# An S4 and spatial-shift mixer kernel: third-order norm roots, the last group's second stage per token row, transfers in two pieces of 64 partitions with all stores on SyncE, fewer idle products

## The chip, the cores and the metric

One core of a Trainium2 chip runs the kernel. The metric is the device time of one execution in microseconds; where several runs are given it is their median. TensorE (PE) multiplies matrices, VectorE (DVE) and ScalarE (ACT) work on tiles, and SyncE (SP) issues transfers, which 16 DMA engines carry out. ACT can issue transfers too.

## The reference

The input is A_u, 2048 tokens of D = 512 numbers. It is normalised per token, goes through a state-space convolution (N = 128 states per channel) and, beside it, through a mixer, and the two are multiplied and added to the input:

```python
def _A_ref(u, ...):                       # 2048-tap convolution by channel
    dt = jnp.exp(log_dt)[:, None]
    P = jnp.exp((dt * A)[:, :, None] * l[None, None, :])       # D x N x L
    K = jnp.einsum("dn,dnl,dn->dl", Cc, P, dt * Bc).real
    y = irfft(rfft(u padded) * rfft(K padded))[:L]
    return y + u * Dskip

def _B_ref(x, w1, w2, w3, w4):
    h = _gelu(_layernorm(x) @ w1)
    # quarters of the channels shifted by +1, -1, +2, -2 tokens
    x1 = x + shifted(h) @ w2
    return x1 + _gelu(_layernorm(x1) @ w3) @ w4                # F = 1376

xn = _layernorm(A_u)
s, g = _A_ref(xn, ...), _silu(_B_ref(xn, w1, w2, w3, w4))
return A_u + s * g
```

## The kernel before

The tile X holds all tokens: partition 64a + 32b + t, and on the free side s = 0 to 15 and the 512 channels. A token's row number in DRAM is made of (t, r, s) with r = 2b + a, so a block of 32 partitions belongs to one r; `ORDER = 0, 2, 1, 3` gives the r of each block.

The work has these stages. `loads` brings in X, the weights and the parameters. X is normalised row by row (s by s): sums of each row (`BN_STATS` to `stats`, `BN_AGGR` to `mv`), a reciprocal root (`rstd`, which takes Newton steps from a first guess), and an affine step. The normalised rows are transposed (xT) and go through w1 and w2 (the products `pb<-xT,w`, `pd<-w,hT`). Beside this the convolution's kernel is made from complex exponentials (`pt`, `mag`, `par`), and both are transformed in stages with scratch in DRAM (`scr_Ud`, `scr_Kda`, `scr_Zda` and others, reloaded as `uin`, `kin`, `zin`). Then the second mixing, `mlp(g)`, runs over groups of two rows s; its products are `pb<-x1T,w3h` and, summed over eleven blocks of F into two accumulators, `pa<-w4h,ghl`, one accumulator for each of the group's two rows. x1T is its transposed input. `inverse` makes the convolution's result from `zin` (products `pd<-zin,is` and `pc<-zin,is`). In `gate`, `inverse` and `finish` the group's X becomes silu(X), is multiplied by the convolution's result, gets the input added (loaded a second time as `xr`, four rows s at a time), and is stored. For the last group `pieces` splits these steps by row, for the others both rows go together.

Every operation is first recorded in a plan. `DUE`, one number for each operation, is the order of priority, and `PIN` says for the operations that ACT or DVE may do which of the two does them; a planner puts the operations of each engine in order by these. Each engine then works through its own list strictly in that order. `E.store` is such a choice too, between SP's queue and ACT's. Where the planner expects PE to wait over 0.8 us, it puts idle products (`pa<-ident`, `pd<-ident`, result not used) ahead of the next operation:

```python
pick.fill = max(0, int((t - start - LEFT) / SPAN))
```

All engines' operations are issued from one helper line, L499 in the kernel before; idle products come from L498. The DMAs on SP share eight semaphores, so a new transfer can be issued when the one eight places earlier has landed.

Of the kernel before, what the change touches and what calls it, by code (L numbers as in the profile page):

```python
# [14 lines left out]
ALU = mybir.AluOpType  # L15
# [9 lines left out]
S = 16  # L25
# [6 lines left out]
INV_2PI = float(np.float32(1.0 / (2.0 * np.pi)))  # L32
QUARTER_PI = float(np.float32(np.pi / 4.0))
# [63 lines left out]
class Op:  # L97
# [20 lines left out]
SPAN, LEFT, LEAST = 0.224, 0.3, 0.8  # L118
# [517 lines left out]
def kernel(  # L636
# [163 lines left out]
    def rstd(dst, var, x, t, by=1.0):  # L800
        V.tensor_scalar(x, var, EPS, None, op0=ALU.add)
        guess(dst, x)
        for f in (1.0, 1.0, by):
            V.scalar_tensor_tensor(t, dst, -0.5 * f, dst, op0=ALU.mult, op1=ALU.mult)
            V.tensor_mul(t, t, x)
            V.scalar_tensor_tensor(dst, t, 1.5 * f, dst, op0=ALU.add, op1=ALU.mult)
# [773 lines left out]
```

## Time and profile before

| what | value |
|---|---|
| time, median of 3 runs | 535.5 us (535.47 to 535.63) |
| the profiled execution's own time | 537.38 us |
| its span | 535.6 us |
| PE busy | 511.1 us, 95% |
| DVE busy | 450.9 us, 84% |
| ACT busy | 400.8 us, 75% |
| DMA on SP's queue | 106.95 MB |
| DMA on ACT's queue | 1.57 MB |
| chain that ended last | PE 68%, DVE 10%, ACT 10%, DMA 7% |

The profile is of one execution; its times are microseconds from the start of its span. The execution's own time is 1.8 us longer than the span, as it includes what lies around it. In a group row, "x16" is the number of instructions, and the name "out<-in" has the program's tiles. "DMA share" is the mean busy share of the 16 DMA engines, PEclk the granted clock of PE.

### The profile page before, as it was taken

How to read it: one execution, taken by the hardware profiler on the slowest of the kernel's cores; microseconds unless marked ns; L12 is line 12 of the kernel's file. 1: busy time of each engine (PE TensorE's matmuls, PEld its weight loads, DVE VectorE, ACT ScalarE, POOL GpSimd, SP SyncE). 2: the span in 40 equal slices, each digit the busy share in tenths (PEclk: the TensorE clock that was granted, in tenths of full speed). 3: DMA queues.
4: the chain of work that ended last, by engine and by line, in shares of the span. 5: the costliest groups of instructions: out<-in, count | busy, mean ns of one | idle time of the engine just before them, and what ended most of it. 6: DMA issues, size and time to landing. Idle time of an engine off the chain costs nothing.

```text
span 535.6 us, 14336 instructions
## 1 busy us (share of the span) xinstructions
PE 511.1 (95%) x6055; PEld 333.1 (62%) x6055; DVE 450.9 (84%) x783; ACT 400.8 (75%) x597; POOL 0.7 (0%) x6
## 2 busy tenths in 40 slices
PE   8789999999999999999999999999999999999992
PEld 8776666774343666565676676666655666566650
DVE  6899999999999999999999999999553267754593
ACT  4999999999998999998989999885336315322420
POOL 0000000000000000000000000000000000000000
PEclk9899999999999999999999999999999999999997
DMA  7994689983886506456333643547989859979986
GB/s 192 258 222 160 227 249 254 281 233 121 296 269 221 101 7 163 140 194 178 112 129 70 180 158 107 118 164 207 251 332 320 282 175 286 258 234 275 310 252 186
DMA packets 95329, 109.44 MB, mean 204 GB/s; under 512 B 40289, under 2 KB 74337, under 8 KB 94369
## 3 DMA queue, kind: packets, MB, share of 16 engines
q1 hardware_dynamic: 94592, 106.95, 69.4%
q10 hardware_dynamic: 672, 1.57, 1.0%
q8 instruction: 47, 0.77, 0.6%
q14 instruction: 18, 0.14, 0.1%
HBM read 64.46 MB, written 37.75 MB: 191 GB/s over the span
## 4 chain that ended last, share of the span: by engine, by line
PE 68%; DVE 10%; ACT 10%; DMA 7%; issue 2%; SPq 2%; ACTq 0%; DVEq 0%
PE pb L499 22%; PE pa L499 22%; PE pd L499 13%; PE pc L499 11%; DVE pt L499 7%; DMA X<-in_A_u_dram 4%; ACT pt L499 3%; SPq L499 2%; ACT ue L499 2%; DVE X L499 1%; ACT L496 1%; DMA scr_Ud<-ue 1%; ACT wst L499 1%; DMA cst<-c_gp 1%; DMA rawC<-in_A_B_re_dram 1%
## 5 line engine op out<-in xcount | busy, mean ns | idle before, releaser
L499 PE MATMUL pb<-x1T,w3h 128*128 128x256 f16 (+1 forms) x1056 | 124.9, 273 | 0.0
L499 PE MATMUL pa<-w4h,ghl 128*128 128x512 f16 (+1 forms) x528 | 123.4, 380 | 0.0
L499 PEld LDWEIGHTS <-w3h 128*128 128x128 f16 (+1 forms) x1056 | 102.6, 100 | 28.8 <-issue 11.6
L499 PEld LDWEIGHTS <-ghl 128*128 128x128 f16 (+1 forms) x528 | 49.4, 98 | 60.6 <-issue 9.2
L499 ACT ACTIVATE g<-pb,wsc 128x512 f32<-128x512 f32 (+1 forms) x48 | 30.7, 650 | 47.6 <-PE pb L499 43.6
L499 ACT ACTIVATE pt<-pt 128x2048 f32<-128x2048 int32 x32 | 61.0, 1908 | 2.4 <-DVE pt L499 2.3
L496 ACT ACT_TABLE_LOAD x48 | 61.6, 1283 | 1.6 <-PEq L1568 0.7
L499 DVE TENSOR_TENSOR pt<-mag,pt 128x1024 f32<-128x1024 f32 x48 | 58.1, 1215 | 0.1
L499 PE MATMUL pd<-w,hT 128*128 128x512 f32 x116 | 53.3, 600 | 2.4 <-DVE X L499 1.9
L499 DVE SCALAR_TENSOR_TENSOR ghl<-g,wsc,ghl 128x512 f16<-128x512 f32 (+1 forms) x48 | 33.5, 700 | 11.6 <-ACT ghl L499 11.3
L499 ACT ACTIVATE mag<-par 128x128 f32<-128x128 f32 x160 | 41.1, 463 | 0.1
L499 ACT ACTIVATE ghl<-g,wsc 128x512 f16<-128x512 f32 (+1 forms) x35 | 24.0, 688 | 20.5 <-PE pa L499 19.0
L499 PEld LDWEIGHTS pd<-w,hT 128*128 128x128 f32 x116 | 21.1, 190 | 27.7 <-issue 23.3
L499 DVE TENSOR_TENSOR pt<-pt 128x2048 f32<-128x2048 f32 x16 | 36.4, 2281 | 0.9 <-ACT pt L499 0.9
L499 PEld LDWEIGHTS pc<-pt 128*32 128x32 f32 x2048 | 29.5, 110 | 8.4 <-issue 5.8
L499 PE MATMUL pc<-pt 128*32 128x64 f32 x2048 | 32.4, 220 | 1.9 <-DVE pt L499 1.0
L499 ACT ACTIVATE pt<-pt,halfpi 128x2048 f32<-128x2048 f32 x16 | 32.0, 1999 | 0.1
L499 PE MATMUL pb<-xT,w 128*128 128x256 f32 x128 | 29.6, 383 | 1.4 <-ACT xT L499 1.4
L499 DVE TENSOR_TENSOR pr<-pd,uin 128x1024 f32<-128x1024 f32 x16 | 19.3, 1219 | 11.5 <-PE pd L499 11.5
L499 PEld LDWEIGHTS pb<-xT,w 128*128 128x128 f32 x128 | 23.6, 190 | 7.8 <-ACT xT L499 3.3
L499 DVE TENSOR_TENSOR pr<-pd,kh 128x1024 f32<-128x1024 f32 x16 | 19.3, 1218 | 6.7 <-PE pd L499 6.0
L499 PE MATMUL pb<-xT,w1h 128*128 128x256 f16 x192 | 22.5, 273 | 0.0
(160 smaller groups left out, 787.8 us busy)
## 6 DMA issues: line engine op xcount, KB each, us to landing
wst<-in_B_w_dram SPq DMA_DIRECT2D x20, 512.0 KB, 5.1
scr_Ud<-ue SPq DMA_DIRECT2D x16, 512.0 KB, 3.9
uin<-scr_Ud SPq DMA_DIRECT2D x32, 256.0 KB, 4.3
cst<-c_gp SPq DMA_DIRECT2D x16, 384.0 KB, 4.0
scr_Uh<-uh SPq DMA_DIRECT2D x8, 512.0 KB, 3.2
scr_Kfa<-k1e SPq DMA_DIRECT2D x8, 512.0 KB, 3.7
kin<-scr_Kfa SPq DMA_DIRECT2D x16, 256.0 KB, 4.1
scr_Zda<-z1e SPq DMA_DIRECT2D x8, 512.0 KB, 5.0
```

The costliest lines, as they stand in the source:

```text
L496: self.engines["ACT"].preload_act_table_set(SETS[table])
L499: ins = [getattr(self.engines[op.eng], name)(*args, **kw).ins for name, args, kw in op.calls]
```

## The change

1. `rstd` takes one third-order step and one Newton step instead of three Newton steps: 7 operations on DVE after the guess instead of 9, in each of eleven calls.
2. The row number is now split as (t, b, a, s), and X, xr and the stores move in two pieces of 64 partitions (one for each a) instead of four of 32. The side in DRAM is then 2 blocks (b) of 32 rows (t). X takes 10 transfers instead of 20, xr 8 instead of 16, the stores 18 instead of 36.
3. All stores are issued by SP; `E.store` is no longer used.
4. In the last group's second stage, the products into the accumulator of the first row are recorded ahead of those of the second row for each block, not alternating, and may be ordered apart.
5. The idle products are counted with a factor of 0.87: 50 instead of 57.
6. `DUE` and `PIN` have other numbers. They set the new order, and some operations go from ACT to DVE.

```diff
+CUBIC = 0.375 ** 0.5, -1.25 / 0.375 ** 0.5, 1.875
...
-SPAN, LEFT, LEAST = 0.224, 0.3, 0.8
+SPAN, LEFT, LEAST, FILLED = 0.224, 0.3, 0.8, 0.87
...
-                    pick.fill = max(0, int((t - start - LEFT) / SPAN))
+                    pick.fill = max(0, int((t - start - LEFT) * FILLED / SPAN))
...
-    xv = u[0].rearrange("(t r s) d -> r t s d", r=4, s=S)
-    ov = out[0].rearrange("(t r s) d -> r t s d", r=4, s=S)
+    xv = u[0].rearrange("(t b a s) d -> a b t s d", a=2, b=2, s=S)
+    ov = out[0].rearrange("(t b a s) d -> a b t s d", a=2, b=2, s=S)
...
-        for f in (1.0, 1.0, by):
-            V.scalar_tensor_tensor(t, dst, -0.5 * f, dst, op0=ALU.mult, op1=ALU.mult)
-            V.tensor_mul(t, t, x)
-            V.scalar_tensor_tensor(dst, t, 1.5 * f, dst, op0=ALU.add, op1=ALU.mult)
+        V.scalar_tensor_tensor(t, dst, CUBIC[0], dst, op0=ALU.mult, op1=ALU.mult)
+        V.tensor_mul(t, t, x)
+        V.scalar_tensor_tensor(t, t, CUBIC[1], t, op0=ALU.add, op1=ALU.mult)
+        V.scalar_tensor_tensor(dst, t, CUBIC[2], dst, op0=ALU.add, op1=ALU.mult)
+        V.scalar_tensor_tensor(t, dst, -0.5 * by, dst, op0=ALU.mult, op1=ALU.mult)
+        V.tensor_mul(t, t, x)
+        V.scalar_tensor_tensor(dst, t, 1.5 * by, dst, op0=ALU.add, op1=ALU.mult)
...
     def by_r(sb, dr, to_dram=False):
-        for r in range(4):
-            a, d = sb[32 * r : 32 * r + 32], dr[ORDER[r]]
-            Q.dma_start(d, a) if to_dram else Q.dma_start(a, d)
+        for a in range(2):
+            part = sb[64 * a : 64 * a + 64]
+            Q.dma_start(dr[a], part) if to_dram else Q.dma_start(part, dr[a])
...
-        for x, k in pieces(g):
-            V.tensor_add(X[:, x], X[:, x], xr[q][:, 2 * (g % 2) : 2 * (g % 2) + 2][:, k])
-            for r in range(4):
-                E.store(ov[ORDER[r]][:, x], X[32 * r : 32 * r + 32, x])
+        for x, k, c in pieces(g):
+            V.tensor_add(X[:, x, c], X[:, x, c], xr[q][:, 2 * (g % 2) : 2 * (g % 2) + 2][:, k, c])
+            by_r(X[:, x, c], ov[:, :, :, x][..., c], True)
...
-                with plan.together(cost=DOWN):
-                    for i in range(2):
-                        for lg, lw in ((0, 0), (0, 1), (1, 0)):
-                            T.matmul(accs[i], ...)
+                for some in ((0,), (1,)) if g == GROUPS[-1] else ((0, 1),):
+                    with plan.together(cost=DOWN * len(some) / 2):
+                        for i in some:
+                            for lg, lw in ((0, 0), (0, 1), (1, 0)):
+                                T.matmul(accs[i], ...)
```

In the lists below a row is an instruction with its output and input, the shape of the output, and the number in a row; numbers in names tell buffers apart (w_106 to w_109 are halves of w1 and w2). First, SP in the head, where X, the weights (wst, w) and the parameter Dt are loaded. Before:

```order
L499 DMA X<-in_A_u_dram 32x2048 x5
L499 DMA w_106<-in_B_w_dram 128x2x512
L499 DMA w_107<-in_B_w_dram 128x2x512
L499 DMA X<-in_A_u_dram 32x2048 x2
L499 DMA Dt<-in_A_Dskip_dram 1x2x64
L499 DMA wst<-in_B_w_dram 128x4x256
L499 DMA X<-in_A_u_dram 32x2048
L499 DMA Dt<-in_A_Dskip_dram 1x2x64
L499 DMA X<-in_A_u_dram 32x2048
L499 DMA is_82<-c_is 128x32
L499 DMA X<-in_A_u_dram 32x2048
```

After:

```order
L497 DMA w_107<-in_B_w_dram 128x2x512
L497 DMA X<-in_A_u_dram 64x1x2048 x2
L497 DMA w_106<-in_B_w_dram 128x2x512
L497 DMA X<-in_A_u_dram 64x1x2048
L497 DMA is_82<-c_is 128x32
L497 DMA X<-in_A_u_dram 64x1x2048
L497 DMA Dt<-in_A_Dskip_dram 1x2x64
L497 DMA w_109<-in_B_w_dram 128x2x512
L497 DMA Dt<-in_A_Dskip_dram 1x2x64
L497 DMA X<-in_A_u_dram 64x1x2048
```

Each X transfer now fills 64 partitions instead of 32, there are half as many, and their place among the weights is much the same.

Second, SP at the end, from the loads of xr to the last store. Before:

```order
L499 DMA xr<-in_A_u_dram 32x2048 x5
L499 DMA scr_Zdb<-z1e 128x1024
L499 DMA zin<-scr_Zda 128x4x256
L499 DMA xr<-in_A_u_dram 32x2048
L499 DMA zin<-scr_Zdb 128x4x256 x2
L499 DMA zin<-scr_Zda 128x4x256
L499 DMA zin<-scr_Zdb 128x4x256 x3
L499 DMA xr<-in_A_u_dram 32x2048
L499 DMA zin<-scr_Zdb 128x4x256
L499 DMA xr<-in_A_u_dram 32x2048
L499 DMA zin<-scr_Zdb 128x4x256 x2
L499 DMA zin<-scr_Zda 128x4x256
```

After:

```order
L497 DMA scr_Zdb<-z1e 128x1024
L497 DMA xr<-in_A_u_dram 64x1x2048 x3
L497 DMA zin<-scr_Zda 128x4x256
L497 DMA xr<-in_A_u_dram 64x1x2048
L497 DMA scr_Zdb<-z1e 128x1024
L497 DMA xr<-in_A_u_dram 64x1x2048
L497 DMA zin<-scr_Zda 128x4x256
L497 DMA zin<-scr_Zdb 128x4x256 x8
L497 DMA zin<-scr_Zda 128x4x256
L497 DMA out_dram<-X 2x32x1024 x14
L497 DMA out_dram<-X 2x32x512 x4
```

All loads of xr now stand ahead of ten of the eleven zin loads; before, three were among them. SP's list before ends with 22 stores of 32x1024 and 32x512; now it ends with 18 whose shape in DRAM is 2x32x1024 or 2x32x512.

Third, ACT at the end. Before:

```order
L499 DMA out_dram<-X 32x1024
L499 ACTIVATE ghl<-g_485,wsc 128x512
L499 ACTIVATE ghl<-g_487,wsc 96x256
L496 ACT_TABLE_LOAD
L499 ACTIVATE warm<-g_487 96x1
L499 DMA out_dram<-X 32x1024 x5
L499 ACTIVATE X<-X 128x512 x2
L499 DMA out_dram<-X 32x1024
L499 DMA out_dram<-X 32x512
L499 DMA out_dram<-X 32x1024
L499 DMA out_dram<-X 32x512 x3
```

After:

```order
L497 ACTIVATE ghl<-g_485,wsc 128x512
L497 ACTIVATE g_487<-pb_100,wsc 96x256
L494 ACT_TABLE_LOAD
L497 ACTIVATE warm<-g_487 96x1
L497 ACTIVATE ghl<-g_487,wsc 96x256
L497 ACTIVATE X<-X 128x512 x2
```

The stores are gone from ACT's list, which now ends with the last group's two functions.

More of the change, by code (lines that the diff above doesn't have):

```diff
@@ L226 @@
 PIN = (
-    "10111111111111111111111111111111111111111111111110101101101111111100111110010011101111111111101110100000111111"
-    "11111001111100100111011111111111110111111111111111111111111111101011011010101111111111111111111111111111111111"
-    "01110110110101011111111111111111111111101111111011011010111111101101101010111111111111111111111111111101111111"
-    "11111111111111111011010111111111110110101111111111111111111111111111110011111110110101010110111101101010111111"
-    "11111111010101010101010101010101111111111111111111111101101111111111111111111111111111111111111111111111111101"
@@ L232 @@
-    "11111111111111111111111111101101111111111111111111111111111111111111111011011111111111111111111101101111101111"
-    "10111110111110111110111110111110111110111110100110011010000000001111110001111111101111111000111111111111111100"
-    "01111111101111111000111111110101000000000111111000111111110111111100011111111011111110001111111101111111000111"
-    "11111011101111110111111001110111001111001111100111101111110011111001111100111001100111100111110011110111111111"
-    "01111001111100111001111111101111110111111101111110111111101111110111111101111110111111101111110111111101111110"
@@ L237 @@
-    "11111110111111011111110111111010100000000011111100011111111011111110001111111101111111000111111110111111100011"
-    "11111111010000000001111110001111111111111111000111111110111111100011111111011111110001111111101110011111001111"
-    "10111110111111110111111001111001111100111110011111001110011001111001111100111100111110011111001111101111011101"
-    "11110111111001111001111100111110111111011110111101111011111100111101111110011111001111100111111100111100111110"
-    "01111001111100111110011111011111100111110011110011011111111011110011100111011111111111110111111111110111111111"
@@ L242 @@
-    "11111111111111011111111111011111111111011111111111111111111111010000000001111111111111111111111111111111111111"
-    "111111111111111100111111011111111110110111111101101011111111001100111100"
+    "10111111111111111111111111111111111111101101011011111111001111100100111011111111111011101110001111111111100111"
+    "11001001110111111111011111010111111111111111111011111011011010101111111111111111111111111111111111110110110101"
+    "01111111111111111111111111111010110110101111111011011010101111111111111111111111111110011111111111111111111110"
@@ new lines @@
+    "11010111111111110110101111111111111111111111111110001111111011010101011011110110101011111111111111010101010101"
+    "01010101010111111111111111111111110110111111111111111111111111111111111111111111111101111111111111111111111111"
+    "10110111111111111111111111111111111111111011011111111111111111110110110110111110111110111110111110111110111110"
+    "11111011111010011001101000000000111111000111111110111111100011111111111111110001111111101111111000111111110101"
+    "00000000011111100011111111011111110001111111101111111000111111110111111100011111111011101111110111111001110011"
@@ new lines @@
+    "00111101111110111110011111011111101111110011100110011110111111001111001111111110111001111100111001111111101111"
+    "11011111110111111011111110111111011111110111111011111110111111011111110111111011111110111111011111111111111010"
+    "10000000001111110001111111101111111000111111110111111100011111111011111110001111111101010000000001111110001111"
+    "11110111111100011111111011111110001111111101111111000111111110111001111101111110111111110111110111111001111001"
+    "11110011111001111101111101100111100111110111110011111001111100111110111110110011110011111001111011111101111110"
@@ L244 @@
+    "11111101111011111111101111110111110111111011111100111110011111110111110111111001111001111101111111101111111101"
+    "11111110111111110011111100111011111111011110111101111001111111111110111111111110111111111111111111111110111111"
+    "11111111111111111011111111111111111111111110000000001111111111111111111111111111111111111111111111111111111111"
+    "1111111111111111111111111"
 )
@@ L832, in loads @@
     def loads():
-        by_r(X[:, 0:2], xv[:, :, 0:2])
+        by_r(X[:, 0:2], xv[:, :, :, 0:2])
         load_w(w1, w1s, stile)
@@ L842, in loads @@
         for k, (s0, s1) in enumerate(((2, 4), (4, 8), (8, 12), (12, 16))):
-            by_r(X[:, s0:s1], xv[:, :, s0:s1])
+            by_r(X[:, s0:s1], xv[:, :, :, s0:s1])
         load_w(w2, w2s, w2place)
@@ L1192, in gate @@
     def gate(g):
-        for x, _ in pieces(g):
-            A.activation(X[:, x], X[:, x], AF.Silu)
+        for x, _, c in pieces(g):
+            A.activation(X[:, x, c], X[:, x, c], AF.Silu)
     def inverse(hf, g):
@@ L1209, in inverse @@
                 return
-            for x, k in pieces(g):
-                V.tensor_mul(X[:, x], X[:, x], pair[:, k])
+            for x, k, c in pieces(g):
+                V.tensor_mul(X[:, x, c], X[:, x, c], pair[:, k, c])
             return
@@ L1221, in finish @@
             xr[q] = at(xrs.pop(), [P, 4, D], F32, "xr")
-            by_r(xr[q], xv[:, :, 4 * q : 4 * q + 4])
-        for x, k in pieces(g):
-            V.tensor_add(X[:, x], X[:, x], xr[q][:, 2 * (g % 2) : 2 * (g % 2) + 2][:, k])
-            for r in range(4):
-                E.store(ov[ORDER[r]][:, x], X[32 * r : 32 * r + 32, x])
+            by_r(xr[q], xv[:, :, :, 4 * q : 4 * q + 4])
+        for x, k, c in pieces(g):
+            V.tensor_add(X[:, x, c], X[:, x, c], xr[q][:, 2 * (g % 2) : 2 * (g % 2) + 2][:, k, c])
+            by_r(X[:, x, c], ov[:, :, :, x][..., c], True)
     def pow2_scale(cols, dst_s, dst_inv, target):
@@ L1443, in pieces @@
         if g != GROUPS[-1]:
-            return [(slice(2 * g, 2 * g + 2), slice(0, 2))]
-        return [(2 * g + k, k) for k in range(2)]
+            return [(slice(2 * g, 2 * g + 2), slice(0, 2), slice(0, D))]
+        return [(2 * g + k, k, slice(0, D)) for k in range(2)]
     def mlp(g):
@@ L1476, in mlp @@
                 fn = FT[j][1]
-                with plan.together(cost=DOWN):
-                    for i in range(2):
-                        for lg, lw in ((0, 0), (0, 1), (1, 0)):
-                            T.matmul(
-                                accs[i], ghl[:fn, lg, a, i * P : (i + 1) * P], w4t[jp][:fn, a, lw],
-                                start=j == 0 and lg == 0 and lw == 0,
-                                stop=j == len(FT) - 1 and lg == 1,
-                            )
+                for some in ((0,), (1,)) if g == GROUPS[-1] else ((0, 1),):
+                    with plan.together(cost=DOWN * len(some) / 2):
+                        for i in some:
+                            for lg, lw in ((0, 0), (0, 1), (1, 0)):
+                                T.matmul(
+                                    accs[i], ghl[:fn, lg, a, i * P : (i + 1) * P], w4t[jp][:fn, a, lw],
+                                    start=j == 0 and lg == 0 and lw == 0,
+                                    stop=j == len(FT) - 1 and lg == 1,
+                                )
         if g == GROUPS[-1]:
             A.activation(warm[:fr], g32[:fr, 0, 0:1], AF.Silu)
-        for x, k in pieces(g):
-            V.scalar_tensor_tensor(X[:, x], duo[0][:, k], a4, X[:, x], op0=ALU.mult, op1=ALU.add)
+        for x, k, c in pieces(g):
+            V.scalar_tensor_tensor(X[:, x, c], duo[0][:, k, c], a4, X[:, x, c], op0=ALU.mult, op1=ALU.add)
     def token_mixing():
```

179 rows, old and new, of the table DUE are left out of this document.

## The prediction

> **What bounds the kernel now.** I read the page first, then the busy times by stretch, then the tensors whose transfers change, then the chain at the end.
>
> ```profile
> span 535.6 us, 14336 instructions
> PE 511.1 (95%) x6055; PEld 333.1 (62%) x6055; DVE 450.9 (84%) x783; ACT 400.8 (75%) x597; POOL 0.7 (0%) x6
> core 0: us, PE busy (x) PEld busy (x) DVE busy (x) ACT busy (x) POOL busy (x), PEclk, DMA share, GB/s
> 0.00:40.00 40.00, 33.36 (x224) 30.71 (x224) 33.83 (x123) 32.77 (x87) 0.70 (x6) 0.96 0.96 224
> 40.00:180.00 140.00, 133.64 (x1535) 83.00 (x1536) 137.89 (x266) 136.18 (x188) 0.00 (x0) 1.00 0.78 226
> 180.00:370.00 190.00, 189.76 (x2644) 124.61 (x2643) 186.25 (x264) 175.60 (x255) 0.00 (x0) 1.00 0.47 134
> 370.00:525.00 155.00, 154.15 (x1656) 94.82 (x1653) 89.73 (x129) 55.05 (x69) 0.00 (x0) 1.00 0.89 269
> 390.00:400.00 10.00, 10.00 (x80) 5.52 (x68) 5.62 (x9) 3.23 (x4) 0.00 (x0) 1.00 0.93 375
> 520.00:525.00 5.00, 5.00 (x52) 2.15 (x49) 3.88 (x6) 1.10 (x3) 0.00 (x0) 1.00 0.92 253
> 525.00:530.00 5.00, 0.14 (x8) 0.00 (x0) 3.23 (x5) 1.20 (x2) 0.00 (x0) 0.87 0.58 147
> 530.00:535.60 5.60, 0.00 (x0) 0.00 (x0) 0.00 (x0) 0.00 (x0) 0.00 (x0) 0.50 0.58 169
> ```
>
> There are three stages. In the first 40 us the DMA engines are the full resource (share 0.96, 224 GB/s). From 40 to 180 VectorE and ScalarE both work nearly all of the time (137.9 and 136.2 of 140 us). From 180 TensorE is full until 525 (189.8 of 190, 154.2 of 155). Then 10 us of stores and little else. So a delay that holds up VectorE in the head is not made good: there is no spare time in the middle stage to win it back, and TensorE in the last one starts later by as much.
>
> The input X comes in during the head, the second copy of it (xr) and the result go through the DMA engines in the tail:
>
> ```profile
> L499 SPq DMA_DIRECT2D X<-in_A_u_dram x20: 311/419/472, 5.9 to 34.3; - x20
> L499 DVE BATCH_NORM_STATS2 stats<-X x16: 658/682/694, 11.9 to 49.7; 128x6 f32<-128x512 f32 x16
> DMA to landing us min/median/max: 3.0/6.9/11.0
> ...
> 14.20 9.11 DMA X<-in_A_u_dram
> 23.32 10.98 DMA X<-in_A_u_dram
> ...
> L499 SPq DMA_DIRECT2D xr<-in_A_u_dram x12: 310/420/1402, 478.9 to 501.8; - x12
> L499 PE MATMUL pc<-zin,is x144: 376/376/400, 494.9 to 524.8; 64*32 64x256 f32 x144
> L499 SPq DMA_DIRECT2D zin<-scr_Zdb x8: 359/463/1602, 493.8 to 506.2; - x8
> L499 SPq DMA_DIRECT2D zin<-scr_Zda x3: 359/360/388, 490.1 to 509.5; - x3
> ```
>
> The first column pair of such a row is the shortest, median and longest duration in ns, then the start of the first and the last. X is issued from 5.9 to 34.3 us, lands a median 6.9 us later, and lies on the chain that ends last for 20 us of the head. VectorE takes X in a fixed order, its sixteen statistics from 11.9 to 49.7. In the tail, twelve xr loads go out between 478.9 and 501.8 and eleven zin loads from 490.1; TensorE's last products read zin.
>
> ```profile
> 517.53 6.60 PE pa L499 x30
> 524.13 0.03 issue
> 524.15 0.76 DVE X L499
> 524.94 0.64 ACT X L499
> 527.65 0.69 DVE X L499
> ...
> L499 SPq DMA_DIRECT2D out_dram<-X x22: 314/366/733, 511.5 to 532.9; - x22
> L499 ACTq DMA_DIRECT2D out_dram<-X x14: 321/387/591, 511.5 to 529.4; - x14
> DMA to landing us min/median/max: 1.6/2.2/5.6
> SPq L499 <- DMA out_dram<-X: 9.9, 5, 5.4
> ```
>
> The last addition ends at 528.3, but SP issues its last store at 532.9: it had stood for up to 5.4 us until an earlier store landed.
>
> **The change, part by part.**
>
> *Transfers of 64 partitions.* X, xr and the stores become half as many, of twice the size. The shape on the DRAM side goes from 32 rows to 2 blocks of 32 rows (the lists of SP in the description show it for the stores). The question that decides the time is over how many of the 16 DMA engines such a transfer is laid. Rows for it:
>
> ```profile
> q1 hardware_dynamic: 94592, 106.95, 69.4%
> q10 hardware_dynamic: 672, 1.57, 1.0%
> scr_Uh<-uh SPq DMA_DIRECT2D x8, 512.0 KB, 3.2
> xr<-in_A_u_dram SPq DMA_DIRECT2D x16, 256.0 KB, 5.3
> L499 SPq DMA_DIRECT2D xr<-in_A_u_dram x16: 310/420/1523, 372.4 to 501.8; - x16
> Dt<-in_A_Dskip_dram SPq DMA_DIRECT2D x4, 0.5 KB
> ```
>
> What one engine moves while busy: SP's queue 106.95 MB in 0.694 x 16 x 535.6 us = 18.0 GB/s; ACT's queue, only stores of the result, 1.57 MB in 0.010 x 16 x 535.6 = 18.3 GB/s; the best stretch, 390 to 400, 375 / (0.93 x 16) = 25.2 GB/s. A transfer of 128 rows lands 524 KB in 3.2 us, 164 GB/s, so it is laid over at least seven engines. Transfers whose outermost length is 2 occur in one place, the four Dt loads. Their row has no landing time, and in the trace's semaphore records, which no view lists, they leave three arrivals each where the others leave sixteen. That speaks for two engines, but Dt has only two rows in all, so it does not prove it for 2 x 32 rows. The bounds are two engines at 18.0 GB/s and sixteen as before. I take two, because the outermost length is what Dt shares with the new transfers, and 25.2 GB/s for each, since large pieces with no neighbours are nearest to the stretch with the fewest small ones.
>
> The Trainium skill ("DMA: Bandwidth & Descriptors", section "Why a DMA increments its semaphore by 16 and not by 1") says that a transfer uses the largest number of engines up to 16 that divides the slowest dimension of both sides, and from SP always the lowest-numbered ones. By this rule the new transfers have 2 engines, and all of them the same two, and the sum is the 702 below; by the landing of the 32-row rows it would be 529.6. No row of this case times a transfer of 2 x 32 rows, so the trace neither confirms nor refutes it.
>
> Head: X is 2048 x 512 x 4 B = 4.19 MB. Two engines need 4.19 / 0.0504 = 83 us (116 at 18.0). The rest of the head's traffic, 224 GB/s x 40 us less X = 4.8 MB, lies on all sixteen, 0.30 MB or 12 us on each; I take 8 of it ahead of the last X. From the first issue at 5.9 the last X lands at 97 (89 to 139). Before, it landed by 34.3 + 6.9 = 41.2, and the last statistics began at 49.7. So VectorE is late by 97 - 49.7 = 47 to 97 - 41.2 = 56: I take **+50**, bounds +39 (89 - 49.7) and +98 (139 - 41.2). What waits behind it is all of VectorE's queue, ScalarE with it, and TensorE's entry to the second mixing at 180.
>
> Middle: two of the eight xr loads (the first four of sixteen before, from 372.4) fill the two engines for 1.05 / 0.0504 = 21 us. Every other transfer has shares on these two and lands up to 21 us later (29 at 18.0), while TensorE is full. Bounds 0 and +29; I take **+5**, since the loads behind them are for later use.
>
> Tail: six xr loads now stand ahead of nearly all zin loads on SP. 3.15 MB of xr and 4.19 MB of stores, 7.34 MB over 50.4 GB/s, are 146 us, and the eleven zin loads, 5.8 MB over sixteen, another 14 on each engine. From 478.9 that ends at 639, 103 past the span. The stores can't start until zin, the last products and the additions are through; between the first zin issue and the first store lay 21 us before, and I take 10 of it as a gap: **+113**, bounds +103 and, at 18.0 (204 + 20 + 21 from 478.9), +188.
>
> *All stores on SP.* 18 issues instead of 22, and ACT's 14 are gone from its queue, ahead of nothing but its last functions. The issue itself costs 18 x 0.37 = 6.6 us over 16 us. With sixteen engines the stall of 5.4 us would go: the last landing, 532.9 + 2.2 = 535.1 before, would come at 528.3 + 2 x 0.37 + 2.2 = 531.2, 3.9 us earlier at best; I take **-3**, as one queue does not drain at once; with two engines it is hidden by the transfer itself.
>
> *Last group per token row.* Row 0 ends nine products of 6.60 / 30 = 0.22 us earlier, 2 us. Its evaluation, function and sums then lie under row 1's products, and behind TensorE stay one of each, 0.7 + 0.64 + 0.7 + 0.69 = 2.7 us instead of 4.2: **-1**, hidden too when the stores are late.
>
> *Norm roots and idle products.*
>
> ```profile
> L499 DVE SCALAR_TENSOR_TENSOR rs<-rs 128x4 f32<-128x4 f32 (+2 forms) x66 | 10.2, 154 | 0.4
> L498 PE MATMUL pd<-ident 128*128 128x128 f32 x60 | 8.8, 316 | 0.0
> L498 PE MATMUL pa<-ident 128*128 128x128 f32 x54 | 6.5, 277 | 0.6 <-DVE par L499 0.6
> 21.00:24.50 3.50, 2.54 (x17) 2.34 (x18) 3.50 (x20) 3.50 (x16) 0.00 (x0) 0.86 1.01 255
> 24.50:28.00 3.50, 3.50 (x23) 3.50 (x23) 3.50 (x13) 3.50 (x17) 0.00 (x0) 0.65 1.07 238
> ```
>
> Two operations of 0.154 us go from each of eleven calls, 3.4 us of VectorE, partly ahead of TensorE's entry. Idle products fall from 57 to 50 (each leaves two records): 7 x 15.3 / 57 = 1.9 us where TensorE has work waiting, nothing where it waits anyway. The new order takes some work from ScalarE to VectorE. Together 0 to -4; I take **-2**.
>
> Sum against the profiled execution's span: 535.6 + 50 + 5 + 113 - 2 = 702. The execution's own time is 537.4, the median of the runs 535.5, practically the span, so I leave it at **702**. Low ends together give 674, high ends 851; for the likeliest case I hold 660 to 800, as not all high ends come together.
>
> **The rivals.** (1) The transfers are laid over sixteen engines as before. For it speaks that the same bytes in rows of the same length landed spread out in every row above that has a landing. Then X comes no later, and the sum is 535.6 - 3 - 1 - 2 = **529.6**: faster. It decides the case from the point where the pieces have enough engines for X to land by 41: 4.19 MB in 35 us, 120 GB/s, five engines at 25.2. (2) Spread out, but the single queue of SP backs up: a store's issue waits for one of the earlier ones, and the tail drains at the 169 GB/s of the last row, winning only the idle products and the roots, 535.6 - 2 = 533.5. Against it, half as many issues. (3) Spread out, but fewer idle products let the clock down in the head: it already fell to 0.65 in 24.5 to 28. One such stretch costs 3.5 x 0.35 = 1.2 us, and it takes six more of them to eat up the gains and give 537.5; TensorE is not the bound there, so this is unlikely. (4) The gains sit in time nobody waits for: 535.5.
>
> **How the numbers follow.** Two engines 0.66, and the predicted time is that case's 702; the Dt records are the only ones with the same outermost length, and rival 1 keeps 0.25 because two rows can't show it. Rival 2 0.03, rival 3 0.03, rival 4 0.03. A difference under 0.2% can't be told from none here. Faster: 0.25 + 0.03 = 0.28; same 0.03; slower 0.66 + 0.03 = 0.69. The likeliest case's range of 660 to 800 leaves over 0.4 out with its own tails, so the range reaches down to rival 1, 527.
>
> **What would show it.** With two engines the DMA share of the first 90 us falls to about 2/16 with near 50 GB/s after the other loads are in, VectorE waits for X, the last statistics begin near 97, TensorE waits for X and then, after xr, for zin; and the last 80 us hold stores alone. With sixteen, X's landing stays near 7 us, the statistics end by 50, and the profile ends some 3 us behind the last addition. I am wrong if those loads land in a few us each.

## The result, and the profile after

The changed kernel takes 730.6 us (median of 4 runs, 727.9 to 733.5) against 535.6 before (median of 4 runs): a ratio of 1.363, with a 95% interval of 1.357 to 1.369. The forecast was 702, for the case of two engines. The profiled execution has a span of 728.4 us.

The page after, with the slices of TensorE, its clock and the DMA engines, and the busy times by stretch:

```profile
span 728.4 us, 14216 instructions
PE 527.0 (72%) x6041; PEld 339.0 (47%) x6041; DVE 458.4 (63%) x777; ACT 388.0 (53%) x581; POOL 0.7 (0%) x6
PE   6246079999999999999999994699999803191000
PEclk9567579999999999999999998799999955596555
DMA  3412336998686346533636354988696122551111
0.00:40.00 40.00, 19.76 (x117) 18.83 (x118) 16.30 (x59) 17.07 (x48) 0.70 (x6) 0.73 0.38 112
40.00:100.00 60.00, 22.60 (x102) 17.52 (x101) 23.55 (x84) 20.41 (x48) 0.00 (x0) 0.64 0.23 76
600.00:640.00 40.00, 12.16 (x100) 5.08 (x101) 3.29 (x6) 0.69 (x1) 0.00 (x0) 0.59 0.43 136
700.00:728.40 28.40, 0.00 (x0) 0.00 (x0) 0.00 (x0) 0.00 (x0) 0.00 (x0) 0.50 0.12 47
```

The work of the engines is nearly the same (VectorE 458 us against 451, TensorE 527 against 511, part of it at a lower clock), but TensorE's slices show three holes: in the first 100 us, near 450, and from 570 on. In the last 28 us nothing runs but stores: a DMA share of 0.12, which is 1.9 of 16 engines, and 47 GB/s, so 47 / (0.12 x 16) = 24.5 GB/s for one engine.

The tensors whose transfers were changed, in the same kernel (first and last start, as before), X here up to 115 us and xr from 500 on:

```profile
L497 DVE BATCH_NORM_STATS2 stats<-X x16: 661/684/695, 26.0 to 110.2; 128x6 f32<-128x512 f32 x16
L497 SPq DMA_DIRECT2D X<-in_A_u_dram x10: 517/784/3296, 4.4 to 83.8; - x10
L497 SPq DMA_DIRECT2D xr<-in_A_u_dram x6: 504/558/11211, 557.4 to 603.0; - x6
L497 SPq DMA_DIRECT2D zin<-scr_Zdb x8: 371/1344/7120, 621.7 to 637.6; - x8
L497 SPq DMA_DIRECT2D out_dram<-X x18: 512/4715/10049, 641.9 to 714.0; - x18
```

And the waits and the pieces of the chain that answer to them:

```profile
DVE stats L497 <- DMA X<-in_A_u_dram: 57.4, 5, 23.4
PE pc L497 <- DMA zin<-scr_Zda: 29.9, 1, 29.9
PE pd L497 <- DMA zin<-scr_Zda: 17.8, 1, 17.8
PE pd L497 <- issue: 16.5, 1, 16.5
9.99 21.91 DMA X<-in_A_u_dram
34.55 14.46 SPq L497
49.05 31.97 DMA X<-in_A_u_dram
83.78 21.67 DMA X<-in_A_u_dram
```

A chain row has its start, its length and what it was; SPq is SP's queue, here SP issuing a transfer. VectorE waits 57 us for X, in five waits. The last X lands at 83.8 + 21.7 = 105.5 and the last statistics begin at 110.2 instead of 49.7. In the tail TensorE stands 29.9 and 17.8 us for zin, which went out behind xr; the stores begin at 641.9.

The delay can be cut at two marks. TensorE's first product with x1T starts the second mixing; the first of the last six (before, twelve) xr loads, at 478.9 before and 557.4 after, comes when the middle is over:

```profile
L499 PE MATMUL pb<-x1T,w3h x264: 272/273/283, 183.6 to 255.7; 128*128 128x256 f16 x120, 128*96 128x256 f16 x12
L497 PE MATMUL pb<-x1T,w3h x71: 272/273/282, 243.4 to 259.9; 128*128 128x256 f16 x71
```

(The first row is before, the second after; both up to 260 us.) Head: 243.4 - 183.6 = 59.8. Middle: 557.4 - 478.9 - 59.8 = 18.7. Tail: 728.4 - 535.6 - 78.5 = 114.3. Together 192.8.

### The profile page after: what moved, and what is told of

Read it like the earlier page. It is cut to its first block, busy times and chain, and to the rows that moved or that the text cites. A ratio compares the mean times of both kernels' runs of the same rounds, so it can differ in the third digit from the quotient of the medians.

```text
span 728.4 us, 14216 instructions
## 1 busy us (share of the span) xinstructions
PE 527.0 (72%) x6041; PEld 339.0 (47%) x6041; DVE 458.4 (63%) x777; ACT 388.0 (53%) x581; POOL 0.7 (0%) x6
## 4 chain that ended last, share of the span: by engine, by line
PE 51%; DMA 16%; DVE 11%; SPq 7%; issue 4%; ACT 1%; DVEq 0%
PE pb L497 17%; PE pa L497 16%; DMA X<-in_A_u_dram 10%; PE pd L497 10%; PE pc L497 8%; SPq L497 7%; DVE pt L497 7%; DMA zin<-scr_Zda 4%; DMA cst<-c_gp 2%; DVE X L497 1%; DVE x2s L497 1%; DVE stats L497 1%; DVE pab L497 0%; DVE ue L497 0%; DVE w3h L497 0%
## 5 line engine op out<-in xcount | busy, mean ns | idle before, releaser
L497 PE MATMUL pa<-w4h,ghl 128*128 128x512 f16 (+1 forms) x528 | 126.8, 385 | 0.8 <-DVE X L497 0.8
L497 DVE BATCH_NORM_STATS2 stats<-X 128x6 f32<-128x512 f32 x32 | 21.5, 683 | 57.4 <-DMA X<-in_A_u_dram 57.4
L497 PE MATMUL pb<-xT,w 128*128 128x256 f32 x128 | 33.4, 417 | 13.3 <-DMA w<-in_B_w_dram 13.3
L497 PEld LDWEIGHTS pb<-xT,w 128*128 128x128 f32 x128 | 26.2, 213 | 20.2 <-issue 16.5
L497 DVE TENSOR_TENSOR X<-X,pd 128x1024 f32<-128x1024 f32 (+1 forms) x15 | 14.5, 969 | 32.9 <-PE pd L497 32.8
L497 PE MATMUL pd<-kin,cst 64*32 64x256 f32 x512 | 18.4, 397 | 17.9 <-issue 16.5
L497 PE MATMUL pc<-zin,is 64*32 64x256 f32 x144 | 6.2, 413 | 29.9 <-DMA zin<-scr_Zda 29.9
```

The costliest lines, as they stand in the source:

```text
L497: ins = [getattr(self.engines[op.eng], name)(*args, **kw).ins for name, args, kw in op.calls]
```

## The experiments

### All transfers in 32 rows again (rows32)

The edit, shortened to what it does:

```diff
     def by_r(sb, dr, to_dram=False):
         for a in range(2):
-            part = sb[64 * a : 64 * a + 64]
-            Q.dma_start(dr[a], part) if to_dram else Q.dma_start(part, dr[a])
+            with plan.together():                 # still one entry of the plan
+                for b in range(2):
+                    part = sb[64 * a + 32 * b : 64 * a + 32 * b + 32]
+                    Q.dma_start(dr[a, b], part) if to_dram else Q.dma_start(part, dr[a, b])
```

> The changed kernel with X, xr and the stores cut into pieces of 32 partitions again (32 rows on the DRAM side, two transfers issued one after the other where the change has one); roots, second stage, idle products, order and stores on SP stay. Theory (two engines carry a transfer of 2 x 32 rows): all 193 us of the span go, and with them the last X lands near 41 us, statistics end by 50; what is left of the change shows, between 528 and 534, estimate 530 from the prediction's rival 1 plus up to 4 for 36 issues on one queue. Rival (the new order or the 18 stores on one queue cost the time, or pieces waiting longer on SP): stays over 600.

Measured: 537.6 us, ratio to before 1.0037 (1.0011 to 1.0063), span 534.3. The statistics of X are where they were:

```profile
L497 DVE BATCH_NORM_STATS2 stats<-X x16: 659/684/695, 12.3 to 49.8; 128x6 f32<-128x512 f32 x16
```

So the whole of the loss, 193 us, lies in how the three tensors are cut. The ratios from here on are to runs of the kernel before in the same series, whose medians were 536.5, 537.0 and 537.4 us, not to the 535.6 above. The estimate of 530 for what is left of the change was a miss: it is not faster than before. The runs called joint take that up.

### One tensor at a time in 64 partitions (x64, xr64, st64)

The edit is rows32 with the cut of the change for one of the three.

> As rows32, but X is loaded in the ten pieces of 64 partitions; xr and stores in 32. Theory: only the head is late, by the 60 us that lie between the last statistics of the two traces (110.2 - 49.7): 590. SP's issues of X and of what follows take several us each. Rival (the three tensors hinder each other, the head alone is made good by later slack): under 560.

> As rows32, but only xr in pieces of 64 partitions. Theory: two of its loads hold up the middle by 22 us, as the trace of the changed kernel has it (xr's third load 82 us later than before, 60 of it the head's); the other six, 3.15 MB at 49 GB/s, take 64 us from about 501 and the zin loads wait behind them until 580; TensorE's rest and the stores, now spread out, need some 25 more: 605. Rival (xr is needed late and is hidden by the inverse): under 550.

> As rows32, but only the stores in pieces of 64 partitions. Theory: 4.19 MB over two engines at 24.5 GB/s are 86 us from the first store at about 510: 596. Rival (SP's issue is the limit, about 4.7 us for each of 18 whatever the engines): the same 595, so this run tells only whether the three parts add up to the whole; their sum would be 60 + 75 + 66 = 201 against 199.

Measured, one run each: 595.6, 604.5 and 598.7 us, so +58.0, +66.9 and +61.1 over rows32's 537.6; expected were 590, 605 and 596. The sum, 186, stands against 193 for the change, which has all three. One line of each, in this order (x64's wait, xr64's wait, st64's stores):

```profile
DVE stats L497 <- DMA X<-in_A_u_dram: 55.7, 5, 23.6
PE pc L497 <- DMA zin<-scr_Zda: 27.7, 1, 27.7
L497 SPq DMA_DIRECT2D out_dram<-X x18: 511/4702/10051, 511.9 to 582.4; - x18
```

Each alone brings the wait that it has in the changed kernel: X holds up VectorE, xr holds up zin and by it TensorE, and the stores run on for 66 us after the last addition's end at 531.2. None is hidden, against the rivals of x64 and xr64. The rival of st64, SP's issue as the limit, gives the same time and isn't decided by it; what bears on it is the DMA share while st64 only stores:

```profile
540.00:590.00 50.00, 0.00 (x0) 0.00 (x0) 0.00 (x0) 0.00 (x0) 0.00 (x0) 0.50 0.13 53
```

That is two engines of 16 (2/16 = 0.125) at work all of the time, so it is they that were full.

### The same pieces with other outermost lengths (spell2, spell4, spell8)

These tell apart whether the size and number of the transfers or their outermost length is the cause. All pieces have 32 rows; only X's side in DRAM is named differently. Row t of a piece then goes to another partition in X than in xr and the stores, so these three kernels leave out the right pairing of tokens and don't give the reference's result; lengths, counts and bytes are those of rows32. The edit, shortened:

```diff
-                    row = dr[a, b]
+                    row = dr[a, b].rearrange("(t h) s d -> h t s d", h=k)   # k = 2, 4, 8
```

> As rows32, 32-row pieces for everything, but X's rows are named in DRAM as 2 blocks of 16, the blocks interleaved (token t of the piece goes to another partition, so the tokens are in another order in X alone; lengths, counts and bytes of all transfers are those of rows32). Theory (the number of engines is the outermost length): X on two engines again, the head late by 60 us as in x64: 590 to 600. Rival (the size of a piece, 64 partitions, or half as many transfers in flight made it slow): as rows32, 537.

> As spell2 with 4 blocks of 8. Theory: four engines at 24.5 GB/s load X in 43 us, and with 12 us of other work on them the last X lands near 60 instead of 41; the statistics end some 5 later instead of at 50: +15, 552, between 545 and 557. Rival (size or count): 537. Rival (anything with two dimensions in DRAM is slow): as spell2.

> As spell2 with 8 blocks of 4. Theory: eight engines load X in 21 us beside 12 of other work, landing by 38, in time for VectorE, which was busy until 50 anyway: 537, at most 541. Rival (two dimensions in DRAM are slow): as spell2.

Measured, one run each: 594.9, 555.2 and 538.0 us; expected 590 to 600, 552 and 537. VectorE's waits for X and the statistics, in the order 2, 4, 8:

```profile
DVE stats L497 <- DMA X<-in_A_u_dram: 55.1, 5, 23.4
DVE stats L497 <- DMA X<-in_A_u_dram: 14.6, 5, 7.4
DVE stats L497 <- DMA X<-in_A_u_dram: 2.4, 3, 1.3
L497 DVE BATCH_NORM_STATS2 stats<-X x16: 659/685/695, 16.8 to 67.5; 128x6 f32<-128x512 f32 x16
L497 DVE BATCH_NORM_STATS2 stats<-X x16: 657/683/695, 13.8 to 51.4; 128x6 f32<-128x512 f32 x16
```

(The last two rows are spell4 and spell8.) With the same twenty transfers of the same bytes, 2 blocks cost what the change's ten large pieces cost (594.9 against 595.6), 4 blocks under a third of it, 8 next to nothing. Size and number are out, and so is "two dimensions are slow": it is the outermost length. That it acts through the number of engines can be read from stretches in which X comes in and hardly any other engines are at work, one for each run, in the order 2, 4, 8:

```profile
84.00:90.00 6.00, 0.00 (x0) 0.00 (x0) 0.00 (x0) 0.00 (x0) 0.00 (x0) 0.50 0.12 51
28.00:32.00 4.00, 4.00 (x34) 3.69 (x32) 4.00 (x19) 2.67 (x9) 0.00 (x0) 0.96 0.25 102
24.00:28.00 4.00, 3.75 (x29) 3.52 (x27) 4.00 (x17) 3.73 (x12) 0.00 (x0) 0.85 0.51 197
```

The DMA shares of 0.12, 0.25 and 0.51 are 1.9, 4.0 and 8.2 engines of 16, and the last number of each row, in GB/s, grows with them: some 24 to 27 for one engine. The rule quoted in the prediction (the Trainium skill, "DMA: Bandwidth & Descriptors", "Why a DMA increments its semaphore by 16 and not by 1") gives 2, 4 and 8 engines here, and these three runs agree with it; that they are the lowest-numbered ones no run here shows.

### What is left of the change (joint, joint_fill, joint_newton, joint_act)

The end of the chain in rows32 shows why the split by token row gives nothing (start us, us, what):

```profile
522.04 2.06 PE pa L497 x9
524.13 0.76 DVE X L497
524.93 0.81 PE pa L497 x3
525.74 1.11 PE pc L497 x32
526.94 0.70 DVE X L497
527.67 1.30 DVE X L497 x2
528.99 0.69 DVE X L497
PE pa L497 <- DVE X L497: 0.8, 1, 0.8
```

Row 0's sum ends at 524.1, only three products ahead of row 1's, and these three wait 0.8 us until VectorE has read row 0's result (the last row is from the list of waits). joint lets the products of both rows alternate again:

```diff
-                for some in ((0,), (1,)) if g == GROUPS[-1] else ((0, 1),):
...
-                        for i in some:
-                            for lg, lw in ((0, 0), (0, 1), (1, 0)):
...
+                both = [(i, lg, lw) for lg, lw in ((0, 0), (0, 1), (1, 0)) for i in range(2)]
+                for some in (both[:3], both[3:]) if g == GROUPS[-1] else (both,):
...
+                        for i, lg, lw in some:
...
```

> As rows32, but in the last group the products of both accumulators alternate again within each block, so both rows end together. In rows32's trace the last three products of row 1 wait 0.8 us for row 0's evaluation, and the last addition ends at 529.7, 1.4 later than before. Theory (that wait cost what the split won): the last addition comes within 0.5 us of rows32's, and the time stays at a ratio of 1.000 to 1.005 to before. Rival (the split won 1 us, as predicted): 1 us longer than rows32.

Measured: 536.2 us, ratio 0.9986 (0.9971 to 1.0002), span 533.4. Its chain ends so:

```profile
520.58 4.01 PE pa L497 x18
524.61 0.76 DVE X L497
525.40 0.64 ACT X L497
526.06 0.70 DVE X L497
526.78 1.30 DVE X L497 x2
528.10 0.69 DVE X L497
```

The last addition begins at 528.1, 0.9 earlier than in rows32: more than the 0.5 expected, and the ratio too lies below the 1.000 to 1.005 expected; both are on the side away from the rival. The first store is issued at 510.4 in rows32 and at 510.5 in joint, so the 0.9 arises in the last 20 us, where the split acts. The two intervals to before do not overlap, so undoing the split makes the kernel faster. The split lost time; it did not win the 1 us predicted. Of the 1.4 us between the medians (537.6 and 536.2) these traces show only the 0.9: four of rows32's twelve runs took over 540 us, none of joint's, and no profile shows what such a run spends the time on. The ratios alone would not show the cause, since joint_fill below moves about as far for a reason not found; it is the 0.9 in the traces that speaks for the split.

The three others start from joint. joint_fill has `FILLED = 1.0`. joint_newton has the three Newton steps in each root, 22 operations more. joint_act issues the stores of the second half of the partitions from ScalarE:

```diff
+            if to_dram and a == 1:
+                ...  plan.add({"ACT": (ISSUE, call)}, ...)
```

> As joint, with the factor on idle products 1.0 again (56 instead of 50). In the first 40 us the granted clock was 0.91 in rows32 and 0.96 in joint and before. Theory (idle products lie in time that TensorE waits anyway, and VectorE bounds the head): the ratio to before within 0.002 of joint's 0.9986. Rival (fewer idle products let the clock down and cost time, rival 3 of the prediction): faster than joint by 1 to 2 us, ratio 0.995 to 0.997.

> As joint, with three Newton steps in each root (22 more VectorE operations of 0.154 us, 3.4 us in all). Theory (VectorE bounds the time up to the first second-mixing product, at 183 us): part of the 3.4 us comes back, half of the calls lie ahead of it, so 1 to 2 us slower than joint, ratio 1.000 to 1.003. Rival (the operations lie beside other work): same as joint, 0.9986.

> As joint, with the stores of one half of the partitions issued by ScalarE. In joint's trace SP issues its last store at 530.7, 1.9 us behind the last addition at 528.8, eight stores of 0.42 us one after the other. Theory (SP's issue is what the tail waits for): the last issue moves to within 0.9 of the last addition, 1 us faster than joint, ratio 0.995 to 0.998. Rival (ScalarE's own work behind the stores is held up by their waits): no gain or a loss of about 1.

| kernel | median us | ratio to before, 95% interval |
|---|---|---|
| joint_fill | 538.9 | 1.0029 (1.0002 to 1.0055) |
| joint_newton | 537.3 | 1.0001 (0.9981 to 1.0021) |
| joint_act | 534.5 | 0.9954 (0.9938 to 0.9969) |

joint_fill isn't faster than joint, as the rival needed, but neither is it the same: its interval begins where joint's ends, at 1.0002, and its runs spread from 534.7 to 542.0. Why more idle products should cost time isn't settled. Its granted clock in the first 40 us is 0.96, that of joint and before, so the clock is not the reason. joint_newton lies between, its interval overlapping joint's; a gain of the roots of about 1 us fits, and none fits too. In the traces its first product with x1T begins at 184.0, joint's at 183.3. joint_act is faster than the kernel before, and than joint by intervals that only just part (0.9969 and 0.9971):

```profile
L497 SPq DMA_DIRECT2D out_dram<-X x18: 314/326/1265, 511.3 to 530.0; - x18
L497 ACTq DMA_DIRECT2D out_dram<-X x18: 321/375/1327, 511.3 to 530.0; - x18
528.87 0.69 DVE X L497
```

With two queues the last stores are issued at 530.0, 0.4 us after the last addition's end at 529.6; in joint the last of 36 on SP went out at 530.7, 1.9 after 528.8. So the stores did wait for SP's issue, and with 36 stores all on SP is worse than half and half. Against the kernel before, with 22 on SP and 14 on ACT, it is no loss: the span ends 4.6 us behind the last addition's end in joint, and 7.3 before (535.6 - 528.3). The profiled spans of joint and joint_act, 533.4 and 533.1, differ by less than the medians; the rest of the difference these traces don't explain.

## Why the prediction was right, and where its sizes were off

The case was right: two engines. The sum was 702, measured 728.4 in the span; most of the 26 us between are the head's 10 and the middle's 14. The range, 527 to 800, reaches over both cases, sixteen engines and two, so that the time lies in it says little. What bears the prediction out are the signs that it named beforehand: a DMA share of 0.13 and 52 GB/s from 80 to 90 us, VectorE's waits for X, TensorE's for zin behind xr, and an end of stores alone, for 67 us where 80 were forecast. Its chance of 0.66 for two engines rested on the four Dt loads, with no row of a 2 x 32 transfer; the spelled runs show what the Dt loads could not.

- **Rate of one engine**: taken 25.2 GB/s, measured 24.5 in the stretch with stores alone. The choice of the best stretch over the mean of 18.0 was right; large pieces on two engines run at nearly that rate.
- **Head**: taken +50, measured +59.8, x64 alone +58.0. Two things were missed. The last X landed at 105.5, not 97. SP issued X's last piece only at 83.8 instead of 34.3, because its issues took long (below), but that is not shown to have cost anything: in none of the stretches of 10 us from 10 to 100 is the DMA share under 0.13, so nothing shows the two engines without work. At 24.5 GB/s for each, X alone takes 86 us from its first issue at 4.4; the 15 us left up to 105.5 are, by this estimate, other transfers' shares of the two engines, where the prediction took 8. And VectorE began the last statistics 4.7 us after the landing, as it takes four rows, with work between them.
- **Middle**: taken +5, bounds 0 and 29, measured +18.7. This is the term that failed most. The prediction said that the loads behind the two xr pieces were for later use. They were not: TensorE stood 16.5 us (`PE pd <- issue`), up to a product with kin at 462.1, of the 21 us that the two engines were full. The trace names nothing that it waited for, so which load it was stays open; but xr64, where only xr is cut so, has the same wait (16.0) and rows32 has none. The mark of the last six xr loads agrees: 496.4 in xr64, and 478.5 for the last twelve in rows32, 17.9 apart.
- **Tail**: taken +113, measured +114.3. It is right in sum, and its order too (xr, zin, products, then stores). zin waited twice: at SP, which issued it between 572.8 and 639.4, and behind xr in the engines. The two loads on which TensorE stood went out at 572.8 and 603.6, and it went on at 610.1 and 635.1, 37 and 31 us later; before, no zin load took more than 10.9 to land.
- **Rival 1**, 529.6 with sixteen engines, had three terms. -3 for the tail nearly held, even with the 36 stores of rows32: its span ends 4.6 us behind the last addition's end (534.3 and 529.7), before 7.3, so 2.7 were won; but that addition ends 1.4 later than before. Two pieces of 64 partitions on sixteen engines were not tried, since X's layout gives such a piece two lengths in DRAM, 2 and 32. -1 for the split was wrong in sign: the prediction had row 0 end nine products earlier, the trace has three, and a wait of 0.8. -2 for roots and idle products: the second mixing began at 182.9 in rows32 against 183.6, a gain of 0.7 up to there.
- **Rival 3** (the clock): rows32 had a granted clock of 0.91 in the head, before 0.96, but joint with the same idle products has 0.96 too, and joint_act, the fastest, 0.91: neither do fewer of them fix the clock, nor does this clock fix the time. (The rival's own figure is off: six more stretches make seven of 1.2 us, 538 and not 537.5.)

## What to carry to other kernels

Look at the outermost length of both sides of a transfer before its size: here pieces twice as large, half as many, took an eighth of the engines, and the planner's cost, which divides by sixteen engines whatever the shape, could not show it. When a shape names two dimensions in DRAM, put the long one outermost or cut the transfer along the short one; for X, 4 x 8 rows cost 18 us and 2 x 16 rows 57, where 8 x 4 cost nothing that could be measured in one run. In this kernel, a split that lets half of the work end early would pay only if the other half does not wait for the first one's reader.

## What the runs showed of the hardware that was not expected

SP's issuing instruction itself took longer while the engines of its transfers were behind. Before, a store's issue on SP took a median of 0.37 us and 0.73 at most; in the changed kernel it took a median of 4.7 us and 10.0 at most, and the one issue of a 16 KB table in the head 14.5 us (the chain's `34.55 14.46 SPq`). A store of 262 KB over two engines at 24.5 GB/s takes 5.3 us, so SP seems to be held to the rate at which the two engines drain; which limit holds it was not tested. What follows from it is shown: other transfers on the queue went out late too. The zin load at 572.8 took 9.8 us to issue, where 1.6 was the most before, and one x1T load 10.4 us at 450.7, where 2.2 was the most.
